# Interleaving weight conversion with the first batch of attention, and attention in eleven steps between feed-forward matmuls

## The chip, the cores and the metric

The kernel runs on one core of a Trainium2 chip. The metric is the device time of one execution in microseconds (us), median of several; lower is better. A run counts as faster or slower than another from 2% on. A ratio of two kernels is the mean time of one kernel's runs over that of the other's of the same rounds, so it is not quite the ratio of the medians that are quoted.

## The reference

Eight batches of linear attention with eight heads feed a gated feed-forward layer:

```python
kv  = einsum('bhsd,bhse->bhde', k, v)            # b=8, h=8, s=576, d=64
out = einsum('bhsd,bhde->bhse', q, kv)
out = out / sqrt(mean(out*out, axis=-1) + 1e-6) * g_norm
x   = out.transpose(0, 2, 1, 3).reshape(4608, 512)
y   = (sigmoid(x @ w_gate) * (x @ w_val)) @ w_out  # 512 -> 1536 -> 512
```

q, k and v are fp32. The three weights arrive as float64. The kernel gets their bits as int64 and makes fp32 of them itself.

## The kernel before

There are 36 weight units of 128 x 512 (gate and value for each of the 12 slices f of the hidden layer, then 12 of w_out). A unit costs five VectorE instructions, two of GpSimd and one of ScalarE:

```python
def convert(u):
    ...
    vec.scalar_tensor_tensor(out=yf, in0=a, scalar=HI_MIN, in1=xf, op0=ALU.is_ge, op1=ALU.mult)            # L120
    vec.tensor_scalar(out=z, in0=y, scalar1=0x07FFFFFF, scalar2=3, op0=ALU.bitwise_and, ...)               # L122
    vec.scalar_tensor_tensor(out=y, in0=y, scalar=0xC0000000, in1=z, ...)                                  # L123
    vec.tensor_scalar(out=z, in0=y, scalar1=0xFF800000, scalar2=None, op0=ALU.bitwise_and)                 # L125
    vec.scalar_tensor_tensor(out=zf, in0=lo, scalar=2.0 ** -52, in1=zf, op0=ALU.mult, op1=ALU.mult)        # L126
    limit(u + 1)                                     # GpSimd L106 and ScalarE L108, of the next unit
    ...
    nc.gpsimd.tensor_tensor(out=flat, in0=zf, in1=yf, op=ALU.add)                                          # L130
    load_unit(u + NST)
```

Attention of a batch works on four pairs of heads, each in four steps: kv (matmuls, VectorE copies the result), q (transposes, ScalarE copies), u (products; square on ScalarE, sum on VectorE, root on ScalarE, reciprocal and norm on VectorE), and x (transposes; ScalarE writes xT). The main program does the first batch alone, then runs the feed-forward by chunks of 512 rows, and between its steps puts one attention step of a later batch and the conversions that the next slice needs:

```python
limit(0)
for step in attention(0):
    step()
convert(0)
convert(1)
done = 2
...
todo = [(0, s) for s in ffn_in(0)] + [(1, s) for s in ffn_in(1)] + [(1, s) for s in ffn_out(0) + ffn_out(1)]
for c in range(2, NG):
    todo += [(c, s) for s in ffn_in(c) + ffn_out(c)]
for i, (c, step) in enumerate(todo):
    ...
    if ahead:
        ahead.pop(0)()
    while done < min(2 * i + 4, 2 * NFT) or i >= NFT and done < min(NFT + i + 2, len(units)):
        convert(done)
        done += 1
    step()          # slice f: 16 first-layer matmul instructions, sigmoid, and gv = value * sigmoid on VectorE
```

PSUM holds two attention tiles of two banks and four feed-forward tiles of one.

## Time and profile before

| | before |
|---|---|
| median of the runs | 1302.28 us (1301.61 to 1303.0) |
| span of the profiled run | 1298.5 us |
| TensorE, VectorE, ScalarE busy | 96%, 23%, 20% |
| mean granted TensorE clock | 0.985 |
| first feed-forward matmul | 54.57 us |
| TensorE full, without a stop, from | 182.11 us |

These are three runs; with a fourth, taken later, the median is 1302.64, which stands beside the result below. The prediction shows the lines behind this. The way to read it: matmuls fill TensorE from 182 us to the end, so only the time before can be won or lost. TensorE's whole work is 1112.5 us of feed-forward and 8 x 13.6 us of attention, 1221.3 together; the last matmul ends at 1293.93, so 72.6 us are idle or slow-clock time.

### The profile page before, as it was taken

Reading aid. Unit: us, or ns where it says so; the run is one execution under the profiler, and the core shown is the slowest. Engines: PE = TensorE matmul, PEld = TensorE weight load, DVE = VectorE, ACT = ScalarE, POOL = GpSimd, SP = SyncE. Lnnn points to the kernel's source line nnn. Section 1 sums busy time; section 2 is a strip of 40 time slices with the busy share of each in tenths; the row PEclk is TensorE's granted clock in tenths of the full one; section 3 lists DMA queues with packets and bytes.
Section 4 is the critical chain, followed back from the end, with each engine's and each line's share of the span. In section 5 each row is a group of like instructions: output and inputs, shape, how many; then the busy total and the mean of one; then the engine's idle time right before and its main releaser. Section 6 shows DMA issues by size and latency. Waiting matters only on the chain.

```text
span 1298.5 us, 10116 instructions
## 1 busy us (share of the span) xinstructions
PE 1242.4 (96%) x4128; PEld 599.2 (46%) x4128; DVE 292.8 (23%) x451; ACT 254.2 (20%) x417; POOL 108.1 (8%) x114
## 2 busy tenths in 40 slices
PE   4688879999999999999999999999999999999998
PEld 3443344444444544444444444444444444444443
DVE  1699955520001110111011101110111001000100
ACT  2323332321012211221122112211122110000000
POOL 1366623300000000000000000000000000000000
PEclk8699989999999999999999999999999999999999
DMA  8254423200021102111111011110200000000000
GB/s 188 76 153 138 133 78 117 77 18 25 24 63 28 28 17 62 28 28 26 44 46 28 18 43 37 29 27 24 63 1 1 25 9 0 1 24 9 1 8 25
DMA packets 62350, 57.29 MB, mean 44 GB/s; under 512 B 40800, under 2 KB 53088, under 8 KB 62304
## 3 DMA queue, kind: packets, MB, share of 16 engines
q1 hardware_dynamic: 56960, 37.76, 11.5%
q0 software_dynamic: 5184, 18.88, 4.5%
q8 instruction: 33, 0.54, 0.2%
q14 instruction: 13, 0.11, 0.0%
q10 hardware_dynamic: 160, 0.00, 0.0%
HBM read 47.19 MB, written 9.44 MB: 44 GB/s over the span
## 4 chain that ended last, share of the span: by engine, by line
PE 88%; DVE 8%; issue 1%; DMA 1%; ACT 1%; SPq 0%; POOL 0%; DVEq 0%; ACTq 0%
PE mm L244 52%; PE mm L264 29%; PE at L197 3%; DVE cy L123 2%; PE at L176 2%; DVE cz L122 2%; DVE cy L120 2%; PE at L216 1%; DVE cz L125 1%; PE at L187 1%; DMA v<-in_v_dram 1%; DVE xn L208 1%; DVE gv L248 1%; DVE ms L204 0%; DMA q<-in_q_dram 0%
## 5 line engine op out<-in xcount | busy, mean ns | idle before, releaser
L244 PE MATMUL mm<-xT,wg 128*128 128x512 f32 x864 | 395.5, 601 | 11.4 <-POOL wg L130 11.4
L244 PE MATMUL mm<-xT,wv 128*128 128x512 f32 x864 | 389.5, 593 | 5.9 <-POOL wv L130 5.9
L264 PE MATMUL mm<-wo,gv 128*128 128x512 f32 x864 | 375.4, 592 | 0.0
L244 PEld LDWEIGHTS mm<-xT,wv 128*128 128x128 f32 x864 | 163.2, 190 | 216.4 <-issue 197.8
L264 PEld LDWEIGHTS mm<-wo,gv 128*128 128x128 f32 x864 | 162.3, 190 | 195.2 <-issue 195.2
L244 PEld LDWEIGHTS mm<-xT,wg 128*128 128x128 f32 x864 | 158.4, 191 | 182.9 <-issue 167.7
L248 DVE TENSOR_TENSOR gv<-mm,sg 128x512 f32<-128x512 f32 x108 | 74.6, 691 | 611.2 <-PE mm L244 611.1
L246 ACT ACTIVATE sg<-mm 128x512 f32<-128x512 f32 x108 | 64.4, 596 | 352.2 <-PE mm L244 352.0
L266 ACT COPY out<-mm 128x512 f32<-128x512 f32 x36 | 21.1, 586 | 330.9 <-PE mm L264 275.2
L204 DVE TENSOR_REDUCE ms<-sq 96x12 f32<-96x768 f32 x32 | 30.3, 948 | 168.6 <-ACT sq L203 168.6
L197 PEld LDWEIGHTS at<-kv,qT 128*96 128x96 f32 x384 | 50.5, 180 | 14.6 <-issue 13.6
L197 PE MATMUL at<-kv,qT 128*96 128x128 f32 x384 | 53.2, 294 | 0.3 <-ACT xT L224 0.3
L180 DVE COPY kv<-at 64x64 f32<-64x64 f32 x64 | 14.2, 221 | 153.7 <-PE at L176 151.7
L203 ACT ACTIVATE sq<-at 96x768 f32<-96x768 f32 x32 | 25.8, 807 | 94.0 <-PE at L197 94.0
L224 ACT ACTIVATE xT<-at,g_col 128x288 f32<-128x288 f32 (+8 forms) x96 | 33.5, 421 | 54.5 <-PE at L216 54.5
L216 PE MATMUL at<-ident,xn 96*128 96x96 f32 x192 | 23.3, 261 | 20.7 <-DVE xn L208 20.7
L108 ACT ACTIVATE ca<-st 128x512 f32<-128x512 f32 x36 | 24.5, 680 | 94.6 <-DVE cy L120 46.3
L106 POOL TENSOR_SCALAR cx<-st 128x512 f32<-128x512 f32 x36 | 32.6, 906 | 95.6 <-DVE cy L120 88.7
L176 PEld LDWEIGHTS at<-v,k 96*64 96x64 f32 x768 | 27.6, 149 | 27.1 <-issue 24.7
L176 PE MATMUL at<-v,k 96*64 96x64 f32 x768 | 32.1, 238 | 6.3 <-DMA v<-in_v_dram 6.3
L123 DVE SCALAR_TENSOR_TENSOR cy<-cy,cz 128x512 uint32<-128x512 uint32 x36 | 37.1, 1031 | 1.2
L189 ACT COPY qT<-at 128x576 f32<-128x576 f32 x32 | 20.4, 638 | 86.4 <-PE at L187 86.4
(27 smaller groups left out, 350.1 us busy)
## 6 DMA issues: line engine op xcount, KB each, us to landing
k<-in_k_dram SPq DMA_DIRECT2D x32, 288.0 KB, 3.3
v<-in_v_dram SPq DMA_DIRECT2D x32, 288.0 KB, 3.8
q<-in_q_dram SPq DMA_DIRECT2D x64, 144.0 KB, 3.0
st<-in_moe_w_gate_dram POOLq DMA_DIRECT2D x12, 512.0 KB, 4.0
st<-in_moe_w_val_dram POOLq DMA_DIRECT2D x12, 512.0 KB, 4.3
st<-in_moe_w_out_dram POOLq DMA_DIRECT2D x12, 512.0 KB, 3.6
out_dram<-out SPq DMA_DIRECT2D x24, 192.0 KB, 2.3
out_dram<-out SPq DMA_DIRECT2D x24, 128.0 KB, 2.4
```

What stands on the lines that cost most here:

```text
L106: nc.gpsimd.tensor_scalar(out=x.bitcast(FP32), in0=hi.bitcast(FP32), scalar1=HI_MAX, scalar2=-HI_MAX, op0=ALU.min, op1=ALU.max)
L120: vec.scalar_tensor_tensor(out=yf, in0=a, scalar=HI_MIN, in1=xf, op0=ALU.is_ge, op1=ALU.mult)
L123: vec.scalar_tensor_tensor(out=y, in0=y, scalar=0xC0000000, in1=z, op0=ALU.bitwise_and, op1=ALU.bitwise_or)
L176: nc.tensor.matmul(ps[HD * e:HD * e + HD, 0, 0:HD], kin[:, e, js], vin[:, e, js], start=(j == 0), stop=(j == NJ - 1))
L197: nc.tensor.matmul(ps[0:NP, j // JH, c0:c0 + P], qT[m][:, j // JH, NP * (j % JH):NP * (j % JH) + NP], kvs[m % 2], start=True, stop=True)
L204: nc.vector.tensor_reduce(out=ms.rearrange("p i n -> p (i n)"), in_=sq.rearrange("p i (n d) -> p (i n) d", d=HD), axis=AX.X, op=ALU.add)
L216: nc.tensor.transpose(ps[:, j // JH, c0:c0 + NP], xn[m][:, j // JH, P * (j % JH):P * (j % JH) + P], ident[0:NP, 0:NP])
L224: nc.scalar.activation(out=chunk(c)[:, m, o:o + n], in_=ps[:, i, r:r + n], func=AF.Copy, scale=g_col)
L244: nc.tensor.matmul(ps, w[name, f][:, m, :], xT[c][:, m, :], start=(m == 0), stop=(m == NMT - 1))
L246: nc.scalar.activation(out=sg, in_=pg, func=AF.Sigmoid)
L248: nc.vector.tensor_tensor(out=gv[c, f], in0=pv, in1=sg, op=ALU.mult)
L264: nc.tensor.matmul(ps, gv[c, f][:, P * t:P * t + P], w["wo", f], start=(f == 0), stop=(f == NFT - 1))
```

## The change

The intent: fill VectorE's idle time in the first batch with conversion, let the first batch's pairs overlap in all eight PSUM banks, and cut attention into eleven steps that go between the feed-forward matmuls, so that each engine has work while another is busy. A unit's conversion is cut into thirds s0, s1, s2. The core of the diff, with cuts marked:

```diff
-        x = sb.tile([P, UW], U32, tag="cx", name="cx", bufs=1)
-        a = sb.tile([P, UW], FP32, tag="ca", name="ca", bufs=1)
+        x = sb.tile([P, UW], U32, tag="cx", name="cx")        # now two buffers
+        z = sb.tile([P, UW], U32, tag="cz", name="cz")
 ...
+    with tc.tile_pool(name="psum0", bufs=4, space=bass.MemoryType.PSUM) as psum0:
+        steps = [attention(n, ...) for n in range(NHP)]
+        for t in range(NHP + 2):
+            kv, qq, uu, xx = t, t, t - 1, t - 2
+            if kv < NHP:
+                for i in range(4):
+                    steps[kv][i]()        # kv_mm, kv_out, q_mm, q_out
+            if 0 <= xx < NHP:
+                steps[xx][9]()            # x_mm
+                steps[xx][10]()           # x_out
+            if 0 <= uu < NHP:
+                steps[uu][4]()            # u_mm
+                steps[uu][5]()            # u_square
+                convert_some(2)
+                steps[uu][6]()            # u_sum
+                steps[uu][7]()            # u_root
+            convert_some(2)
+            if 0 <= uu < NHP:
+                steps[uu][8]()            # u_norm
 ...
-        return psum.tile([P, 2, 512], FP32, tag="at", name="at")           # 2 buffers
-        return psum.tile([P, 512], FP32, tag="mm", name="mm", bufs=4)
+        psum.tile([P, 2, 512], FP32, tag="at", name="at")                  # 1 buffer
+        return psum.tile([P, 512], FP32, tag="mm", name="mm", bufs=6)
 ...
+    def first_layer(c, f0=0, f1=NFT):
+        for f in range(f0, f1):
+            converted(2 * f + 1)
+            pg, pv = mm_ps(), mm_ps()
+            for ps, name in ((pg, "wg"), (pv, "wv")):
+                for m in range(NMT):
+                    nc.tensor.matmul(ps, w[name, f][:, m, :], xT[c][:, m, :], ...)
+                    if m % 2:
+                        slot()            # the next attention step, if there is one
+ ...
+            nc.vector.tensor_tensor(out=gv_tile(c, f), in0=pv, in1=sg, op=ALU.mult)
+            convert_some(6)
 ...
+    feed(1)
+    first_layer(0)
+    flush()
+    feed(2)
+    first_layer(1, 0, NFT // 2)
+    second_layer(0)
+    first_layer(1, NFT // 2, NFT)
+    second_layer(1)
```

gv has 18 buffers in place of 24. The number of conversions, matmuls and bytes is the same.

## The prediction

> **What bounds the kernel now.** I read the page's busy tenths first, then stretches by window, then the chain of waits around their borders, then the timeline of single engines. In the page:
>
> ```profile
> PE   4688879999999999999999999999999999999998
> ...
> DVE  1699955520001110111011101110111001000100
> ```
>
> TensorE is full from the sixth slice on; VectorE is full in slices three to five and nearly free later. By stretch (start:end, length, busy us with instructions of PE, PEld, DVE, ACT, POOL, granted clock, DMA share, GB/s):
>
> ```profile
> 90.00:110.00 20.00, 16.71 (x69) 7.92 (x68) 18.93 (x28) 7.40 (x10) 12.35 (x12) 1.00 0.45 136
> ...
> 164.00:180.00 16.00, 8.40 (x40) 5.95 (x41) 4.95 (x7) 4.55 (x8) 0.46 (x1) 0.89 0.10 33
> ...
> 498.60:635.85 137.25, 137.25 (x483) 66.48 (x481) 18.59 (x32) 28.21 (x47) 0.00 (x0) 1.00 0.13 34
> ```
>
> So there are three regimes: conversion of the weights on VectorE, a short drain of attention, then a TensorE that never waits. The chain shows the borders (start us, us, what):
>
> ```profile
> 53.41 1.39 DVE cz L122
> ...
> 161.89 0.70 DVE cz L126
> 162.67 1.28 POOL wv L130
> 163.99 3.70 PE mm L244 x8
> 167.69 1.32 PE at L197 x12
> ...
> 182.11 7.88 PE mm L244 x16
> ```
>
> and at the end 41.21 us of L264 from 1252.72, so matmuls end at 1293.93.
>
> TensorE's budget follows. 96 second-layer instructions take 41.21 us, 0.429 each. A chunk has 192 first-layer (82.4) and 96 second-layer ones: 123.6; nine are 1112.5. A steady chunk with attention takes 137.2, so attention costs 13.6 a batch, 3.4 a pair. From 182.11 the work left is 8 x 123.6 + 41.2 + 6 x 13.6 = 1111.6, ending at 1293.7, as measured. Hence all that this change can win or lose is TensorE's idle time before 182: 182.1 - 82.4 - 2 x 13.6 = 72.5 us (slow-clock time included).
>
> **What the Trainium skill says.** "PSUM — Partial Sum Buffer", section "Engine vs sequencer instructions", says that the queues of ScalarE and VectorE are strict FIFO. The trace agrees: the first conversion starts at 49.4, though its data was there at 9.5, because attention is ahead of it on VectorE. My argument rests on this. "SBUF — State Buffer", section "Who interferes with whom", says that VectorE with two SBUF inputs, or in a two-port mode, and GpSimd block each other for a whole instruction. It agrees:
>
> ```profile
> 89.61 0.69 DVE L120 SCALAR_TENSOR_TENSOR cy<-ca,cx 128x512 f32<-128x512 f32 x1
> 90.33 1.38 DVE L122 TENSOR_SCALAR cz<-cy 128x512 uint32<-128x512 uint32 x1
> ```
>
> L122 takes 1.38 while GpSimd's sum runs (89.78 to 91.43), 0.43 otherwise. "TensorE: Matmul & The Clock Gate", section "Part 1: The HAM clock gate", says that the array falls to half clock after an idle window of about 3.4 us, until about as long a busy one. The granted clock after the gap of 3.92 us that ends at 172.92 agrees (the first 22 us, shown at 1.00, don't):
>
> ```profile
> 174.00:176.00 2.00, 2.00 (x11) 1.82 (x9) 0.00 (x0) 0.69 (x3) 0.00 (x0) 0.50 0.00 0
> ```
>
> At 54.57, after such gaps, eight first-layer matmuls took 5.11 us in place of 3.43: 1.7 us lost a cold start.
>
> **The change part by part.** The arithmetic is the same on every engine: 36 conversions with five VectorE instructions each, the same matmuls, the same bytes. Only order and buffers move.
>
> Conversion rate: from one gv to the next, both without attention (66.62 to 75.71), are 9.09 us for two units and a gv of 0.69, so 4.2 us a unit, 1.4 a third. With its ring of two cx the range limit may start earlier, but GpSimd's L106 already follows its load at once there; I expect 8.5 us for six thirds.
>
> First batch. Now its loop is transposes, products, square, sum, root, norm, some 8 us a pair at half clock; its xT is complete at 51.9 and the first matmul at 54.57 awaits the first weight. After: 20 thirds (6.7 units, some 28 us of VectorE work) run inside it. Four PSUM buffers save the wait of the products for the copy out (about 1 us a pair). But two thirds stand between sum and norm, so 2.7 us of VectorE lie on the loop where 0.6 us of root lay. Loading is unchanged (second k and v at 15.8), and the first norm ends near 27.8. A loop is transposes 1.2 + products 2.6 + square 0.9 + sum 1.0 + thirds 2.5 + norm 1.3 = 9.4. Three give 56, and transposes 57: ffn starts at T0 = 57 in place of 54.6.
>
> First layer of chunk 0. Before, VectorE converts f+1 while TensorE does f, and a whole sum-root-norm stands in one step whose transposes come steps later; VectorE never idles, 9.1 us an f. After, six thirds (8.5) follow each gv, and steps whose results TensorE needs at the next slot or the one after (copy of kv, sum, norm) are queued behind them. With one PSUM buffer for attention, q's transposes await the kv copy too. TensorE then stops in the middle of an f; when VectorE releases it, VectorE goes on to this f's gv and waits for TensorE's remaining 1.7 to 5.2 us. Neither overlaps the other there. A slot comes every four instructions, 1.72 us; 11 steps a pair make 2.75 f. Walking this by hand (gv end, absolute):
>
> f0: 6.87 + kv 0.85 + q 0.5 + cold 1.8; gv at 67.8. f1: sum behind 8.5 of thirds; gv 78.0. f2: norm at 87.8 behind thirds, TensorE idle 9.2; transposes, half an f, cold 1.7; gv 94.7. f3: kv copy 103.7, idle 5.5, half an f, cold; gv 110.2. f4: sum, root, norm; 122.1. f5: 131.8. f6: 141.0. f7: norm 152.1 after 7.1 idle; 152.8. f8: 163.2. f9: 173.4. f10: norm 183.2 after 6.9 idle, a quarter f, cold; 188.3. f11: 197.5. Chunk 1: f0 stops at q (5.2 idle); 211.7. f1: 221.9. f2: norm 231.7, 8.3 idle; 238.5. The last four thirds end at 244.2, kv copy 244.7. The 88 thirds after T0 are 125 us of these 188; gv 10, attention 14; the rest, near 38, is VectorE waiting for TensorE.
>
> From 244.7 TensorE has work for 1111.6 less 3.5 f of chunk 1 (24.0) and 1.25 pairs of batch 2 (4.3): 1083.3, ending at 1328.0. The last copy and store (4.6, as before) give a span of 1332.6; timed runs lie 3.8 above the span (1302.28 against 1298.5): 1336. I take off 4 for slack that a walk by hand misses: 1332, 30 us or 2.3% more.
>
> Steady chunks: eleven steps over 48 slots. From products to transposes are five slots, 8.6 us; square 0.81, sum 0.95, table load 1.28, root 0.30, reciprocal 0.22, norm 0.95 and a sigmoid of 0.60 between, with its own table load, are some 7 at worst. One PSUM buffer is enough, nothing waits, the change is worth 0 there. Moving half of chunk 1's first layer behind chunk 0's second, with 18 gv in place of 24, is neutral too: both are full TensorE work.
>
> **Rivals.** (1) The lead of 6.7 units pays: VectorE's 28 us leave the conversion stretch, no stall replaces them, and the 12 units of w_out still hide beside TensorE. Then some 20 to 25 us are won: about 1280. For it: VectorE is at 1 to 6 tenths in the first two slices. Against it: the FIFO order, and w_out's thirds now come at six an f, before they are needed. (2) The coupling is there but without half-clock restarts, and VectorE finds less GpSimd contention: about 10 less from cold starts, 5 from thirds: 1317 to 1321. For it: a restart's clock depends on a window's phase. (3) Steady chunks stall too, since only one pair is in PSUM: 1 us a pair over 23 pairs makes 1355. Against it: the slack of 1.6 us above.
>
> **Range and chances.** The walk has some fifteen synchronisations with an error near 1 us each, partly common (clock, contention), and T0 is sure to about 4; so 1332 with 1309 to 1352 for eight in ten. The 2% line upwards is 1328.3, inside the range and a bit below the middle: 0.58 slower, 0.37 within, and 0.05 faster, which would take rival 1 in full.
>
> **What would show it.** First ffn matmul near 57; VectorE, at 9 tenths or more now between 57 and 162, at 7 to 8 in first_layer(0) with idle put to first-layer matmuls ahead of gv; TensorE idle ahead of the transposes and q's transposes, put to norm and kv copy, some 45 us in all, with granted clock 0.5 behind the gaps; TensorE full only from about 245; chunks of 137.2 after that. I am wrong if TensorE is full by about 210 (then it is rival 1), or if chunks after 360 exceed 138.5 (rival 3).

## The result, and the profile after

The changed kernel takes 1343.37 us (1342.05 to 1344.08, 4 runs) against 1302.64 (1301.61 to 1303.61); the ratio is 1.0312 (95% interval 1.0294 to 1.0329): slower by 3.1%. The predicted time was 1332, the range 1309 to 1352.

The page's busy tenths of the kernel after (40 slices of 33.5 us):

```profile
PE   4577776799999999999999999999999999999998
...
DVE  3577988411001210121011101120112001100100
...
PEclk8688888899999999999999999999999999999999
```

TensorE is now at 7 tenths where it was at 8, fills two slices later (from the ninth; before, from the seventh, not the sixth as the prediction counted), and its clock is below 9 tenths through eight slices. VectorE has more in the first slice, as intended (3 tenths in place of 1; the second has 5 in place of 6), and is busy for longer. By stretch (start:end, length, busy us with instructions of PE, PEld, DVE, ACT, POOL, granted clock, DMA share, GB/s):

```profile
90.00:120.00 30.00, 24.43 (x88) 12.57 (x89) 16.85 (x23) 7.22 (x12) 11.46 (x10) 0.83 0.31 92
...
230.00:250.00 20.00, 10.84 (x48) 5.18 (x46) 13.35 (x18) 4.26 (x8) 6.79 (x6) 0.74 0.18 55
```

In the conversion stretch VectorE was 95% busy before; now it is 56% (16.85 of 30) between 90 and 120, and TensorE isn't full either. TensorE's timeline shows where it stops (start us, us, engine, line, operation, count, and in brackets the idle time before and what ended it). The stops of 1.5 us and more between 57 and 257 us are:

```profile
90.13 1.19 PE L252 MATMUL at<-ident,sq 96*128 96x96 f32 x6 [9.35 <-DVE sq L244]
...
105.86 1.22 PE L212 MATMUL at<-ident,q 96*128 96x96 f32 x6 [5.44 <-DVE kv L205]
...
124.53 0.69 PE L252 MATMUL at<-ident,sq 96*128 96x96 f32 x6 [2.30 <-DVE sq L244]
...
155.42 1.19 PE L252 MATMUL at<-ident,sq 96*128 96x96 f32 x6 [6.40 <-DVE sq L244]
...
189.23 1.19 PE L252 MATMUL at<-ident,sq 96*128 96x96 f32 x6 [7.04 <-DVE sq L244]
...
213.60 1.22 PE L212 MATMUL at<-ident,q 96*128 96x96 f32 x6 [7.28 <-DVE kv L205]
...
239.88 1.20 PE L252 MATMUL at<-ident,sq 96*128 96x96 f32 x6 [9.16 <-DVE sq L244]
...
252.11 0.72 PE L212 MATMUL at<-ident,q 96*128 96x96 f32 x6 [1.73 <-DVE kv L205]
```

All eight are attention's transposes (L252 of the normed values, L212 of q), and each waits for VectorE: for the norm (L244), or for the copy of kv (L205), which empties the one PSUM buffer that q's transposes write to. They add up to 48.7 us. VectorE's timeline shows both halves of the trap around the first of them:

```profile
87.85 1.01 DVE L132 SCALAR_TENSOR_TENSOR cx<-cx,cz 128x512 uint32<-128x512 uint32 x1
88.78 0.21 DVE L242 RECIPROCAL ms<-ms 96x12 f32<-96x12 f32 x1
89.03 0.95 DVE L244 TENSOR_TENSOR sq<-at,ms 96x768 f32<-96x768 f32 x1
96.04 0.69 DVE L326 TENSOR_TENSOR gv<-mm,sg 128x512 f32<-128x512 f32 x1 [6.06 <-PE mm L320]
```

The norm starts only when the last conversion (L132) of the block that began at 80.11 is done; its data, the root, had been ready since 79.92 (on ScalarE, 79.62 and 0.30). Then VectorE itself is idle for 6.06 us, since the next thing in its queue is the gv of the slice in whose middle TensorE stood. The gv's waits for matmuls between 60 and 252 us are 5.40, 6.06, 6.65, 1.11, 4.29, 4.85 and 6.28, together 34.6 us. Neither engine overlapped the other there.

The last stop is released by this line of VectorE's timeline:

```profile
251.60 0.45 DVE L205 COPY kv<-at 64x64 f32<-64x64 f32 x2
```

After it the chain of waits is TensorE alone. At three later borders (start us, us, what):

```profile
951.24 1.72 PE mm L320 x4
...
1088.48 82.40 PE mm L320 x192
...
1294.47 41.22 PE mm L344 x96
```

A chunk with attention takes 1088.48 - 951.24 = 137.24 us, just as before, with one attention buffer in place of two. The last matmul ends at 1335.69: 114.4 us above the 1221.3 of work, against 72.6 before. The difference, 41.8, is the whole loss.

### The profile page after: what moved, and what is told of

It reads as the page before. It is cut to its first block, busy times and chain, and to the rows that moved or that the text cites. A ratio compares the mean times of both kernels' runs of the same rounds, so it can differ in the third digit from the quotient of the medians.

```text
span 1340.3 us, 10165 instructions
## 1 busy us (share of the span) xinstructions
PE 1250.0 (93%) x4128; PEld 602.8 (45%) x4128; DVE 300.2 (22%) x451; ACT 267.7 (20%) x429; POOL 112.0 (8%) x114
## 4 chain that ended last, share of the span: by engine, by line
PE 85%; DVE 8%; issue 2%; ACT 0%; DVEq 0%; ACTq 0%
PE mm L320 51%; PE mm L344 28%; DVE cz L130 3%; PE at L226 2%; DVE cx L132 2%; PE at L199 2%; DVE cx L125 1%; PE at L252 1%; PE at L212 1%; DVE cz L137 1%; DVE gv L326 0%; DVE sq L244 0%; DVE ms L235 0%; DVE cz L138 0%; DVE kv L205 0%
## 5 line engine op out<-in xcount | busy, mean ns | idle before, releaser
L320 PE MATMUL mm<-xT,wv 128*128 128x512 f32 x864 | 402.2, 604 | 0.0
L320 PE MATMUL mm<-xT,wg 128*128 128x512 f32 x864 | 400.4, 602 | 1.2 <-ACT xT L262 1.2
L320 PEld LDWEIGHTS mm<-xT,wg 128*128 128x128 f32 x864 | 161.9, 192 | 186.6 <-issue 184.2
L348 ACT COPY sg<-mm 128x512 f32<-128x512 f32 x36 | 21.1, 586 | 360.2 <-PE mm L344 352.6
L205 DVE COPY kv<-at 64x64 f32<-64x64 f32 x64 | 14.1, 221 | 298.1 <-PE at L199 297.1
L252 PE MATMUL at<-ident,sq 96*128 96x96 f32 x192 | 25.4, 277 | 54.3 <-DVE sq L244 54.3
L252 PEld LDWEIGHTS at<-ident,sq 96*128 96x128 f32 x192 | 22.0, 160 | 71.3 <-issue 68.2
L130 DVE TENSOR_SCALAR cz<-cx 128x512 uint32<-128x512 uint32 x36 | 44.0, 1223 | 1.2
L212 PE MATMUL at<-ident,q 96*128 96x96 f32 x192 | 23.5, 263 | 21.1 <-DVE kv L205 14.5
L132 DVE SCALAR_TENSOR_TENSOR cx<-cx,cz 128x512 uint32<-128x512 uint32 x36 | 39.8, 1106 | 1.2
```

The costliest lines, as they stand in the source:

```text
L130: vec.tensor_scalar(out=z, in0=x, scalar1=0x07FFFFFF, scalar2=3, op0=ALU.bitwise_and, op1=ALU.logical_shift_left)
L132: vec.scalar_tensor_tensor(out=x, in0=x, scalar=0xC0000000, in1=z, op0=ALU.bitwise_and, op1=ALU.bitwise_or)
L212: nc.tensor.transpose(ps[:, j // JH, c0:c0 + NP], pairs[n]["q"][:, j].rearrange("p e d -> p (e d)"), ident[0:NP, 0:NP])
L252: nc.tensor.transpose(ps[:, j // JH, c0:c0 + NP], d["xn"][:, j // JH, P * (j % JH):P * (j % JH) + P], ident[0:NP, 0:NP])
L320: nc.tensor.matmul(ps, w[name, f][:, m, :], xT[c][:, m, :], start=(m == 0), stop=(m == NMT - 1))
```

## The experiments

My theory (A) after the result: the in-order queue of VectorE. Blocks of six conversion thirds stand ahead of small attention steps that TensorE needs at once, TensorE stops in the middle of a slice, and VectorE then has to wait for the rest of that slice. The rivals: (B) one PSUM buffer for attention is too few, whatever the order; (C) VectorE simply has more to do, since each conversion became slower (five instructions of a unit: 4.21 us as the sum of the mean durations, 3.87 before). Eight kernels were run, all with correct results. "Idle" is the end of the last matmul less 1221.3, where the end is the span less 4.6 us, the tail of the last copy and store in both kernels. The four runs x1, x2, x4 and x5 and the four others were timed in two sets of rounds, in which the kernel before took 1302.24 and 1302.14.

| kernel | median us | ratio to before | idle, us |
|---|---|---|---|
| before | 1302.2 | 1 | 72.6 |
| after | 1343.37 | 1.0312 | 114.4 |
| x1_spread | 1305.16 | 1.0022 | 77.8 |
| x2_late | 1312.31 | 1.0076 | 84.3 |
| x4_at2 | 1328.56 | 1.0202 | 100.7 |
| x5_warm | 1336.89 | 1.0266 | (has extra matmuls) |
| x3_both | 1274.25 | 0.9785 | 46.2 |
| x6_nofirst | 1354.42 | 1.0401 | 125.2 |
| x7_first | 1266.41 | 0.9728 | 38.6 |
| x8_align | 1334.91 | 1.0251 | 106.4 |

By the 2% rule x1 and x2 are the same as the kernel before, x3 and x7 faster, x5, x6 and x8 slower; x4 is unclear (interval 1.0187 to 1.0217).

### x1_spread: the same thirds, one or two behind every slot

```diff
                     if m % 2:
                         slot()
+                        convert_some(1 + m // 2)
 ...
             nc.vector.tensor_tensor(out=gv_tile(c, f), in0=pv, in1=sg, op=ALU.mult)
-            convert_some(6)
```

> Changed kernel, but the six conversion thirds of each f are issued one or two behind every slot instead of all six behind the gv. Same work, same lead, same buffers. Theory A (the in-order queue of VectorE: blocks of 8.8 us stand ahead of sum, norm and kv copy, TensorE stops in the middle of an f, and VectorE then waits for the rest of that f): VectorE's 35 us of waits for matmuls in 57 to 252 nearly vanish and the half-clock restarts with them; TensorE is full from about 215, time 1300 to 1316. Theory B (one PSUM buffer for attention is too few, whatever the order of the conversions): the stops stay, 1335 or more. Theory C (VectorE simply has more to do, as each conversion became slower): no change, 1340.

Measured: 1305.16 us, 38.2 less than the change. The stop ahead of the same transposes went from 9.35 us to the first of these lines, and the longest that is left is the last of them (TensorE's timeline of x1_spread):

```profile
82.66 0.69 PE L252 MATMUL at<-ident,sq 96*128 96x96 f32 x6 [1.76 <-DVE sq L244]
92.29 0.71 PE L212 MATMUL at<-ident,q 96*128 96x96 f32 x6 [0.99 <-DVE kv L205]
109.59 0.69 PE L252 MATMUL at<-ident,sq 96*128 96x96 f32 x6 [3.23 <-DVE sq L244]
...
138.40 1.19 PE L252 MATMUL at<-ident,sq 96*128 96x96 f32 x6 [4.63 <-DVE sq L244]
```

All seven stops together are 20.7 us, against 48.7. No gv waits for matmuls before 211 us, and VectorE is busy for 29.09 of the 30 us between 90 and 120, in place of 16.85. Nothing but the place of conversions in the queue differs, with the same buffers and instructions, so A holds for nearly all of the loss and B falls as its main cause. C falls as the main cause too: the five instructions still take 4.08 us a unit. A rival that I had not named falls with it, more work on ScalarE: in the changed kernel and in x1 alike ScalarE loads its function tables 28 times for the root and 28 times for the sigmoid (22 and 22 before), and x1 loses next to nothing. What is left against the kernel before is 3 us.

### x2_late: the blocks stay, w_out is converted in chunk 1

```diff
-            convert_some(6)
+            convert_some(min(6, 6 * NFT - made[0]) if c == 0 else 3)
 ...
-    first_layer(1, 0, NFT // 2)
+    first_layer(1)
     second_layer(0)
-    first_layer(1, NFT // 2, NFT)
     second_layer(1)
```

(and 24 gv buffers)

> Changed kernel with blocks behind the gv as they are, but the twelve w_out units are not converted in chunk 0; they come at three thirds an f in chunk 1, whose whole first layer then stands before both second layers as in the kernel before (24 gv buffers). Theory A: chunk 0's first layer is unchanged up to f9 (gv near 178), then no blocks stand in the way, f11 ends near 195 in place of 206 and chunk 1 stops TensorE for some 5 us only: about 1319 (1311 to 1327). Theory B: the stops in chunk 1 stay (some 18 us): 1330 or more.

Measured: 1312.31 us, 31 less than the change. Up to f7 the stops are those of the change (9.34, 5.46, 2.29, 6.41 us); behind f7 only one of 0.90 us and this one are left:

```profile
213.64 0.69 PE L252 MATMUL at<-ident,sq 96*128 96x96 f32 x6 [1.60 <-DVE sq L244]
```

So pulling w_out's twelve units forward, before anything needs them, at a full block per slice, was most of the loss in the second half of the stretch. It and x1 take away largely the same waits, so the two gains can't be added.

### x4_at2: two attention buffers, four for the feed-forward

```diff
-        return psum.tile([P, 512], FP32, tag="mm", name="mm", bufs=6)
+        return psum.tile([P, 512], FP32, tag="mm", name="mm", bufs=4)
 ...
-            fill.extend(attention(n, lambda: psum.tile([P, 2, 512], FP32, tag="at", name="at")))
+            fill.extend(attention(n, lambda: psum.tile([P, 2, 512], FP32, tag="at", name="at", bufs=2)))
```

> Changed kernel with two attention buffers and four for the ffn, in place of one and six. Theory A: only the stops of q's transposes for the kv copy go (f3 and the first f of chunk 1), which cost VectorE 6.7 and 4.9 us of waiting; the stops of the transposes for the norm stay: about 1331 (1326 to 1336). Theory B (one buffer is the cause): over 25 us are won, under 1318.

Measured: 1328.56 us, 14.8 less. The long stops of q's transposes (5.44 and 7.28 us) are gone; in their place the products, which read kv, wait 1.60 and 3.44 us for the same copy. The stops for the norm are nearly unchanged (9.31, 1.85, 6.43, 7.02 and 8.30 us). The first of each kind:

```profile
89.56 1.19 PE L252 MATMUL at<-ident,sq 96*128 96x96 f32 x6 [9.31 <-DVE sq L244]
105.24 1.52 PE L226 MATMUL at<-kv,qT 128*96 128x128 f32 x12 [1.60 <-DVE kv L205]
```

The single buffer turned VectorE's lateness into stops of q as well; that is the part of B that is true. It does not stand alone: with the order of x1 the single buffer costs far less (its stops at q are 0.99 and 3.48 us), and in x3 and x7 nothing.

### x5_warm: fill the long stops with repeated matmuls

```diff
+    AGAIN = {(0, 2, "wg"): (2, 4), (0, 3, "wg"): (1, 4), (0, 7, "wv"): (1, 4), (0, 10, "wv"): (3, 2),
+             (1, 0, "wv"): (3, 2), (1, 2, "wg"): (2, 4)}
 ...
+                again, n = AGAIN.get((c, f, name), (0, 0))
+                for i in list(range(n)) * again:
+                    nc.tensor.matmul(ps, w[name, f][:, i, :], xT[c][:, i, :], start=(i == 0), stop=(i == n - 1))
                 for m in range(NMT):
```

> Changed kernel with repeated first-layer matmuls (the same products once more, results unchanged) ahead of the six long stops, sized to leave 2 to 3 us of each stop: 64 extra instructions, about 34 us of TensorE's work put into its idle time. Nothing else moves. If the half-clock restarts behind the stops cost time, as my prediction had it, the six restarts go to full clock and some 11 us are won: 1330 to 1335. If they cost nothing, 1343; if the repeats get in the way, more.

Measured: 1336.89 us, 6.5 less, though TensorE does more (72 instructions more by the page's count; I had written 64). Four of the six stops were left with 1.70, 3.00, 1.90 and 2.15 us, and three of these went on at full clock (the fourth partly). Two were left with 2.49 and 2.54 us and still went on at half clock. One of each kind:

```profile
90.16 1.19 PE L252 MATMUL at<-ident,sq 96*128 96x96 f32 x6 [2.49 <-DVE sq L244]
91.14 4.82 PE L325 MATMUL mm<-xT,wv 128*128 128x512 f32 x8
...
105.58 0.71 PE L212 MATMUL at<-ident,q 96*128 96x96 f32 x6 [1.70 <-DVE kv L205]
106.13 3.63 PE L325 MATMUL mm<-xT,wv 128*128 128x512 f32 x8
```

Eight matmuls of one kind take 4.82 us after one stop and 3.63 after the other; in the changed kernel those after the second took 5.47. So the slow restarts do cost time, as predicted. The miss (1330 to 1335 expected) comes from the restarts that stayed cold; two of them at about 1.85 us each (1.19 + 4.63 in the chain, where 0.50 + 3.46 is warm) and some 1 us of the fourth would bring the sum to 11, which is an estimate and not measured.

### x6_nofirst: no conversion inside the first batch

```diff
-                convert_some(2)
                 steps[uu][6]()
                 steps[uu][7]()
-            convert_some(2)
             if 0 <= uu < NHP:
                 steps[uu][8]()
+    convert_some(20)
```

> Changed kernel without conversion inside the first batch: the same 20 thirds stand in one block of some 29 us between the first batch and the ffn; everything after is the same. If conversion inside the first batch is worth its 28 us, 1370; my estimate is less, since it lengthens the loop of sum and norm by about 2 us a pair and the ffn's first f may overlap the block: first f's q waits for the block's end near 77, gv of f0 near 81 in place of 70, time about 1354 (1348 to 1360). If the thirds in the first batch cost more than they win, 1343 or less.

Measured: 1354.42 us. Converting inside the first batch is worth 11 us, not the 28 us of VectorE work that lie there. The feed-forward starts earlier without it, at 51.07, and stops in its first slice:

```profile
74.97 1.22 PE L212 MATMUL at<-ident,q 96*128 96x96 f32 x6 [14.59 <-DVE kv L205]
```

### x8_align: one third more at the start

```diff
                 steps[uu][8]()
+    convert_some(1)
```

> Changed kernel with one more third at the end of the first batch, so that each block begins with a whole unit and the gv stands between the end of one unit and the start of the next, as in the kernel before, beside GpSimd's sum. If the slower conversions (4.2 us a unit against 3.87) come from where GpSimd's sum falls, a block takes 8.3 in place of 8.8, and with 14 blocks some 6 us are won: 1334 to 1339. If they come from the larger ring, 1342.

Measured: 1334.91 us, 8.5 less, for moving every block's boundary by one third (and for one third less to do in the blocks, some 1.4 us). The five instructions of a unit now take 3.68 us in the mean (0.730 + 0.865 + 0.903 + 0.490 + 0.692). The first unit of a block, behind the gv (VectorE's timeline):

```profile
69.09 0.68 DVE L125 SCALAR_TENSOR_TENSOR cx<-cz,cx 128x512 f32<-128x512 f32 x1
69.81 0.43 DVE L130 TENSOR_SCALAR cz<-cx 128x512 uint32<-128x512 uint32 x1
```

In the changed kernel the line L130 took 1.22 us in the mean, since GpSimd's sum of the unit just finished (L143) ran beside the next unit's first two instructions (GpSimd's and VectorE's timelines):

```profile
71.11 1.65 POOL L143 TENSOR_TENSOR wg<-cz,cx 128x512 f32<-128x512 f32 x1 [13.68 <-DVE cz L138]
...
71.66 1.38 DVE L130 TENSOR_SCALAR cz<-cx 128x512 uint32<-128x512 uint32 x1
```

With the boundary between units at the gv, every second sum runs beside gv and attention, which keep their times (in x8 the sum at 76.86 stands beside attention's sum of 0.94 us and a gv of 0.68). So the slower conversions came from where GpSimd's sum falls, and the second cx buffer, which x8 keeps, is not the cause.

### x3_both: spread, w_out late, and the lead spent

```diff
+    def pace(c, done):
+        if c == 0:
+            converted_to = min(6 * NFT, 20 + -(-(6 * NFT - 20) * done // 44))
+        else:
+            converted_to = 6 * NFT + -(-3 * NFT * done // (4 * NFT))
+        convert_some(max(0, converted_to - made[0]))
 ...
                         slot()
+                        pace(c, 4 * f + 2 * (name == "wv") + m // 2 + 1)
 ...
-            convert_some(6)
```

(with the order of chunk 1 and the 24 gv buffers of x2_late)

> Changed kernel with thirds spread over the slots and w_out in chunk 1 only (whole first layer first, 24 gv buffers), and the lead of 20 thirds spent: 52 thirds over the first 44 slots of chunk 0, 4.7 an f, so that VectorE's 8.6 us an f are near TensorE's 8.2. Theory A says that nothing then stops TensorE for long: first layer of chunk 0 from 58 to about 163, full from there, 1284 (1278 to 1292), faster than both. If the lead can't be spent (TensorE bound to VectorE's queue for another reason), 1297 or more.

Measured: 1274.25 us, below the expected 1278 to 1292, and 2.15% below the kernel before (by the ratio). TensorE's timeline has no stop from the first feed-forward matmul on; this one is the last:

```profile
57.80 3.59 PE L327 MATMUL mm<-xT,wg 128*128 128x512 f32 x4 [1.18 <-ACT xT L262]
```

I had reckoned with 1.47 us a third, 4.4 a unit, which would have kept VectorE slightly behind TensorE. But the conversions became cheaper still: the five instructions take 3.34 us a unit (0.804 + 0.630 + 0.738 + 0.469 + 0.701), as GpSimd's sums now mostly fall beside something else than L130. I take this for the reason that the expectation was too high; no run tests it alone.

### x7_first: on top of x3_both, the first batch's thirds moved off its loop

```diff
                 for i in range(4):
                     steps[kv][i]()
+                    if t == 0 and i % 2:
+                        convert_some(3)
 ...
-                convert_some(2)
+                convert_some(3)
                 steps[uu][6]()
                 steps[uu][7]()
-            convert_some(2)
             if 0 <= uu < NHP:
                 steps[uu][8]()
+    convert_some(2)
```

> As x3_both, but the first batch's thirds are where VectorE waits anyway: six in the first pair's loading time, three ahead of each sum (while TensorE and ScalarE work on the pair), none between sum and norm, two at the end: 20 as before. If the two thirds between sum and norm lengthen the loop, as the prediction said (9.4 us against some 7.6), the ffn starts near 50 in place of 58 and the time falls by about 7 more, 1277 (1270 to 1284). If the loop is bound by something else, as x3_both.

Measured: 1266.41 us, 7.8 less than x3_both and 2.72% below the kernel before, so it beats both kernels. The same 20 thirds, with none between sum and norm, and the first matmul of the feed-forward at 49.05 (chain of waits):

```profile
49.05 3.75 PE mm L329 x4
52.81 1.48 PE at L199 x24
54.29 3.94 PE mm L329 x8
```

From there to the end the chain is TensorE alone. The 38.6 us of idle and slow time that remain lie in the first batch, in which TensorE has some 13.6 us of work in 49 us, and in the first cold matmuls.

## Why the prediction was right

The direction and the mechanism were right, and the range holds the result. The size was too small: 30 us forecast, 41 measured. Step by step:

- **TensorE's budget.** It held to the last digit that matters: from the last stop (252.11) TensorE needed 1083.6 us to 1335.69, where the prediction had 1083.3.
- **The first batch.** First norm predicted to end near 27.8; it ended at 27.94. First feed-forward matmul predicted at 57, seen at 58.38. This sum is nearer than its parts, so some of it is luck: the three loops from norm to norm took 8.65, 8.90 and 10.36 us where the prediction had 9.4 each (its terms add to 9.5). The last is long through a wait that the prediction did not have: up to 50.87 VectorE waits 4.32 us for the range limit on ScalarE, which stands behind the square in ScalarE's queue, and attention's sum stands behind that third on VectorE. That the thirds lie on the loop is shown by x7, which moves them and wins 7.8 us. By the timelines the four stretches from sum to norm shrink from 12.8 us to 7.4 in it; that is 5.4 of the 9.3 us by which the feed-forward starts earlier than in the changed kernel, and the rest lies ahead of the sums.
- **The walk through chunk 0.** The stops came where it put them. Predicted 9.2, 5.5, 7.1, 6.9, 5.2 and 8.3 us; measured 9.35, 5.44, 6.40, 7.04, 7.28 and 9.16. The prediction gave no figure for the stop at f4 (2.30) and had none before the last kv copy (1.73); it named some 45 us in all, and 48.7 were measured. Its end times slipped in three places: f0's gv was 2.2 us early (67.8 against 69.97), of which 1.4 is the later start; f3, with its slow restart, added 0.9, and f6 stood at 3.1 (141.0 against 144.14); from f7 on each slice added 0.5 to 0.9, so that f11 was 6.4 early (197.5 against 203.94) and the last kv copy 7.4 (244.7 against 252.05). The term behind the last part is the block of six thirds: 8.5 us predicted, some 8.8 measured early (80.11 to 88.86), which smaller items such as overlapping ends made up for, and 9.2 among w_out's units (178.64 to 187.88, up to the reciprocal). The prediction took the rate from the kernel before, where the gv between two units covers one of GpSimd's sums; it overlooked that with a lead of 20 thirds, which is not a multiple of three, every gv falls inside a unit and covers none. x8 shows this term nearly by itself: one third more at the start, 8.5 us less, of which some 1.4 are the third itself.
- **The 4 us taken off "for slack that a walk by hand misses"** had the wrong sign; the walk itself said 1336.
- **Cold restarts.** Predicted at 1.7 us each, from 5.11 less 3.43; but 5.11 runs to the end of the last matmul and 3.43 from start to start, and like with like (5.11 against 3.60) gives 1.5. Both are too small: in the chain of the changed kernel the restarts at 90.13, 105.86, 155.42 and 189.23 cost some 1.9, 2.5, 3.3 and 1.8 us against the same instructions at full clock (estimates from the chain, transposes included). x5 shows that they are real: 6.5 us won by warming four of six, the rest not measured. The column of granted clock does not show all of this: for the first 22 us of the kernel before it reads 1.00, yet the 24 matmuls of L176 take 1.55 us at 5.37 and at 15.91, and 0.92 at 20.54.
- **Steady chunks.** Predicted worth 0, and 137.2 us a chunk; measured 137.24.
- **Rival 1** (the lead pays, 1280) fails for the change as written, but x3, at 1274, shows that it was the right hope for another order of the same work. **Rival 2** (no cold cost, less contention) is refuted by x5, and by the conversions' 4.21 us. **Rival 3** (steady stalls) by the chunk time.

The check named in the prediction as "VectorE at 7 to 8 tenths in first_layer(0)" holds in the mean only: it was at 56% between 90 and 120 us, and at 96% (28.79 of 30) between 120 and 150, where fewer attention steps fell in mid-slice.

## What to carry to other kernels

On an engine with an in-order queue, the place of long background work counts more than its amount: put it in pieces shorter than the slack of the next small step that another engine waits for, and never as a block ahead of it. Convert or prefetch at the pace of need, so that a lead won early is spent and not rebuilt with work that could wait. When an instruction takes longer beside one of another engine, as L130 did here (1.38 us in place of 0.43), look at what stands beside what: moving a boundary by one third of a unit was worth 8.5 us.

## What the Trainium skill lacked or had wrong

- "TensorE: Matmul & The Clock Gate", section "Part 1: The HAM clock gate", gives an idle window of about 3.4 us before the clock falls. In x5 stops of 2.49 and 2.54 us were followed by slow matmuls (4.82 us for eight, against 3.63; the granted clock is 1.00 between 89 and 90 us, in the first of these stops, and 0.50 between 91 and 92, behind it), and one of 3.00 us wasn't. The page does say that the window is free-running; no run here shows which phase a stop meets, so a stop's length alone doesn't decide.
- "SBUF — State Buffer", section "Who interferes with whom", was right on the conflict: L130, a two-port candidate, took 1.38 us beside GpSimd's sum and 0.43 without. No page says how much that is for a whole kernel, and it is more than one might think: the same five operations of a unit cost 4.21, 3.87, 3.68 or 3.34 us in the mean (changed kernel, kernel before, x8, x3).
